# Attention overlapped with a narrow FFN1: where the additions, casts and loads of its inputs stand

## The chip, the cores and the metric

The kernel runs on one core of one Trainium2 chip. The metric is the device time of one launch in microseconds, lower is better. PE is TensorE, DVE VectorE, ACT ScalarE, POOL GpSimd; SP issues most transfers.

## The reference

```python
# attention: q, k, v are (4, 8, 576, 64); M_prev (4, 8, 64, 64); z_prev (4, 8, 64)
scores = where(causal, -1e9, q @ k.T / sqrt(64))
local = softmax(scores) @ v
q_p = elu(q) + 1
mem_out = (q_p @ M_prev) / (q_p . z_prev + 1e-06)
attn = g * mem_out + (1 - g) * local             # g = sigmoid(beta), one per head
x = attn, heads joined                           # (2304, 512)
x = elu(x @ w1_in) @ w1_out                      # w_in (512, 2048), w_out (2048, 512)
out = leaky(x @ w2_in, 0.01) @ w2_out
```

All is float32. In the FFN each float32 operand is kept as a rounded high part and a low rest, and a product takes three matmuls: high x high, high x low, low x high.

## The kernel before, in words

**Attention.** It goes batch by batch (0 to 3), and in a batch by pairs of heads. `attention_units` writes a list of small units with a cost each: products of scores, transposes of the weights, products with v, and the preparation of the next pair. Batch 0 leaves its result in one scratch array (`xm`). From batch 1 on a pair's result comes in two parts, and each goes through `xp` (DVE, line 529) and a store on SP (line 530) to `xq`; x is the sum of the two parts.

**The narrow part.** Seven of the sixteen blocks of 128 hidden columns of FFN1 run beside attention, for a batch whose attention is done. Its 576 tokens are cut into two halves of 288. A half is a row of units from `phase1_units`:

- `u_x`: from `xm` (batch 0, line 675) or `xq` (lines 681 and 682) SP loads x and y; for `xq` four additions of 128 x 288 on DVE (line 684); four casts to the high part xh on ACT (`split_x`, line 608, in the profile under its helper's line 239) and four subtractions to the low part xl on POOL (line 609); two stores of them.
- `u_h`, seven times, called H below: twelve matmuls (`h_mm`, line 616), then elu on ACT and DVE (lines 628 to 630) and the split of its result (lines 241 and 623).
- `u_o`, four times, called O: 21 matmuls (`o_mm`, line 644), a copy, and the store of ys (line 697).

**The order.** The loop at the end of the code below runs attention's units and counts their cost in `pos`. When a batch's attention is done, its narrow units are put into `fill`, to start at `pos + DELAY`, and from there on each attention unit earns credit with which narrow units are run. They run under `tc.high_priority(offset=FILL_OFF)`, which lets the scheduler pull their instructions some places ahead in the engines' lists. What is left of `fill` when attention ends goes to `side` and is merged with the loading of further weights. Then come the wide part of FFN1 (nine blocks) and FFN2, which the change leaves as they are.

An engine runs its list in order: an instruction that waits holds all those behind it.

Of the kernel before, what the change touches and what calls it, by code (L numbers as in the profile page):

```python
# [8 lines left out]
F32 = mybir.dt.float32  # L9
# [3 lines left out]
ALU = mybir.AluOpType  # L13
# [6 lines left out]
def _f(ap):  # L20
    return ap.bitcast(F32)
# [3 lines left out]
def kernel(  # L25
# [14 lines left out]
    nc = tc.nc  # L40
# [4 lines left out]
    NKC = DM // P  # L45
    NF = DFF // P
    NFA = 7
# [4 lines left out]
    V32 = 1  # L52
# [4 lines left out]
    E_GH, E_WH, E_VH, E_MS, E_V32, E_XH, E_RS, E_Y = "V", "A", "V", "P", "P", "A", "P", "A"  # L57
# [7 lines left out]
    RESERVE = 60000.0  # L65
    EARLY = 150
    DELAY = 13000.0
    NHP = H // 2
    PSUM = bass.MemoryType.PSUM

# [71 lines left out]
    def tile_tok(t):  # L142
        b, ca, cb = t
        r0 = CH[ca][0]
        r1 = CH[cb - 1][0] + CH[cb - 1][1]
        return b * S + r0, r1 - r0

    def halves(n):
        return [(0, n)] if n <= 320 else [(0, n // 2), (n // 2, n // 2)]


    parts = [(i, o, w, tile_tok(t)[0] + o) for i, t in enumerate(tiles1) for o, w in halves(tile_tok(t)[1])]
    xm_scr = [dram.tile([P, NKC, tile_tok(t)[1]], F32, name=f"xm{i}") for i, t in enumerate(tiles1)]
    xq_scr = [
        [dram.tile([P, NKC, tile_tok(t)[1]], F32, name=f"xq{i}_{j}") for j in range(2)] for i, t in enumerate(tiles1)
    ]
    xp_scr = [[dram.tile([P, NKC, p[2]], F32, name=f"x{n}{i}") for i, p in enumerate(parts)] for n in "hl"]
# [8 lines left out]
        out=mask[:, 448:576], in_=mask[:, 448:576], pattern=[[-1, 128]], compare_op=ALU.is_ge,  # L166
        fill=-1e30, base=0, channel_multiplier=1,
# [36 lines left out]
    def bank(tag):  # L204
        return psum.tile([P, 512], F32, tag=tag, bufs=BANKS[tag], name=tag)
# [31 lines left out]
    def copy(eng, dst, src):  # L237
        if eng == "A":
            nc.scalar.copy(dst, src)  # L239
        else:  # L240
            (nc.vector if eng == "V" else nc.gpsimd).tensor_copy(dst, src)  # L241
# [8 lines left out]
    class Pair:  # L250


        def __init__(self, ti, hp):
# [6 lines left out]
            self.full_v = ti < V32  # L260
            self.pad = pads[(ti * NHP + hp) % 2]

# [285 lines left out]
    def attention_units():  # L548

        pairs = [Pair(ti, hp) for ti in range(len(tiles1)) for hp in range(NHP)]  # L550
        keys = [(pr, j, g) for pr in pairs for j in range(2) for g in pr.groups]
# [45 lines left out]
    NW = 288  # L597

    def mtile(tag, bufs, dt=F32, shape=None):
        shape = shape or (NW,)  # L600
        pool = pools.get(("own", tag), pools["mlp"])
        return pool.tile([P] + list(shape), dt, tag=tag, bufs=bufs, name=tag)

    def split_x(xt, w, par):
        xh = mtile(f"xh{par}", 1, F32R, (NKC, NW))[:, :, 0:w]
        xl = mtile(f"xl{par}", 1, F32R, (NKC, NW))[:, :, 0:w]
        for c in range(NKC):
            copy(E_XH, xh[:, c], xt[:, c])
            nc.gpsimd.tensor_tensor(out=xl[:, c], in0=xt[:, c], in1=_f(xh[:, c]), op=ALU.subtract)
        return xh, xl  # L610

    def h_mm(ph, wi, xh, xl):
        n_mm = 0
        for kc in range(NKC):
            for wj, xx in ((0, xh), (1, xh), (0, xl)):
                nc.tensor.matmul(ph, wi[:, wj, kc, :], xx[:, kc, :], start=n_mm == 0, stop=n_mm == 11)  # L616
                n_mm += 1
# [8 lines left out]
    def elu(ph, w):  # L626
        e = mtile("e", EB)[:, 0:w]
        nc.scalar.activation(out=e, in_=ph, func=AF.Relu, scale=-1.0)
        nc.scalar.activation(out=e, in_=e, func=AF.Exp, scale=-1.0)
        nc.vector.scalar_tensor_tensor(out=e, in0=e, scalar=-1.0, in1=ph, op0=ALU.add, op1=ALU.max)  # L630
        return g_split(e, w)
# [7 lines left out]
    def o_mm(py, fs, key, ec, gs, first, last, opens=True, closes=True):  # L639
        for f in fs:  # L640
            wo = wo_tiles[key, f]
            gh, gl = gs[f]
            for n_mm, (wj, gg) in enumerate(((0, gh), (1, gh), (0, gl))):
                nc.tensor.matmul(  # L644
                    py, wo[:, wj, ec * P:(ec + 1) * P], gg,
                    start=opens and f == first and n_mm == 0, stop=closes and f == last and n_mm == 2,
                )
# [5 lines left out]
    def h_bank():  # L653
        nonlocal n_ph
        n_ph += 1
        return bank("tp" if tail and n_ph % 2 else "pm")

    def phase1_units(ti):

        units = []  # L660
        for pi, (pt, o, w, _) in enumerate(parts):
            if pt != ti:
                continue
            st = {}

            def u_x(pi=pi, o=o, w=w, st=st):
                def split():
                    st["x"] = split_x(xt, w, pi % 2)
                    for n in range(2):
                        nc.sync.dma_start(xp_scr[n][pi], _f(st["x"][n]))  # L670
                    st["g"] = {}

                xt = mtile("x", 1, F32, (NKC, NW))[:, :, 0:w]
                if ti < V32:
                    nc.sync.dma_start(xt, xm_scr[ti][:, :, o:o + w])
                    split()
                    return
                x2 = mtile("y", 1, F32, (NKC, NW))[:, :, 0:w]
                for j in range(2):
                    ps, pz = slice(64 * j, 64 * j + 64), slice(64 - 64 * j, 128 - 64 * j)  # L680
                    nc.sync.dma_start(xt[ps], xq_scr[ti][j][ps, :, o:o + w])
                    nc.sync.dma_start(x2[ps], xq_scr[ti][j][pz, :, o:o + w])
                for c in range(NKC):
                    nc.vector.tensor_tensor(out=xt[:, c], in0=xt[:, c], in1=x2[:, c], op=ALU.add)
                split()

            def u_h(f, w=w, st=st):
                ph = h_bank()[:, 0:w]
                h_mm(ph, wi_tiles[0, f], *st["x"])
                st["g"][f] = elu(ph, w)  # L690

            def u_o(ec, pi=pi, w=w, st=st):
                py = bank("sc" if tail else "pm")[:, 0:w]
                o_mm(py, range(NFA), 0, ec, st["g"], 0, NFA - 1)
                y = mtile("st", 2)[:, 0:w]
                copy(E_Y, y, py)
                nc.sync.dma_start(y_scr[pi][:, ec], y)

            units.append((0, u_x))
            for f in range(NFA):  # L700
                units.append((HC * 12 * w / 2.4, lambda f=f, u=u_h: u(f)))
            for ec in range(NKC):
                units.append((3 * NFA * w / 2.4, lambda ec=ec, u=u_o: u(ec)))
        return units

    def merge(a, bu):
        ta = sum(c for c, _ in a) + 1.0
# [14 lines left out]
    def close_decode():  # L722
        wst_a.__exit__(None, None, None)
        pools["decode_bank"] = None
        pools["outer"] = tc.tile_pool(name="mlpx", bufs=1, reuse_waits="tile", side="left")
        early = pools["outer"].__enter__()
        for tag in ("x", "y", "xh0", "xl0"):
            pools["own", tag] = early
        pools["own"] = tc.tile_pool(name="mlp", bufs=1, reuse_waits="tile", side="left")
        pools["mlp"] = pools["own"].__enter__()  # L730
# [17 lines left out]
    c_mlp = NFA * 24 * NT / 2.4  # L748
    rate = (c_mlp - RESERVE) / (c_att - DELAY)
    dec = [lambda f=f: load_w(0, wpa, w1i, w1o, f, f) for f in range(NFA)]  # L750
    fill = []
    credit = pos = 0.0
    for c, u, done in att:
        u()
        pos += c
        while dec and pos >= c0 * DSPAN * (NFA - len(dec)) / NFA:
            with tc.high_priority(offset=0):
                dec.pop(0)()
        if done == 0:
            close_decode()  # L760
        if done is not None:
            fill += [(pos + DELAY, c2, u2) for c2, u2 in phase1_units(done)]
        if fill and fill[0][0] <= pos:
            credit += c * rate
        while fill and fill[0][0] <= pos and fill[0][1] <= credit:
            _, c2, u2 = fill.pop(0)
            credit -= c2
            with tc.high_priority(offset=FILL_OFF):
                u2()
# [95 lines left out]
    for gi, (t0, w) in enumerate(wide):  # L865
        pos = {}
# [24 lines left out]
        for tb in range(w // P):  # L891
            r0 = t0 + tb * P
            for hf in range(2):
                cs = slice(hf * DM // 2, (hf + 1) * DM // 2)
                o = mtile("st", 2, F32, (DM // 2,))
# [32 lines left out]
```

## Time and profile before

| | |
|---|---|
| median of 3 runs | 1095.66 us (1095.63 to 1100.39) |
| profiled execution | 1098.26 us, span 1096.2 us, mean granted clock 0.995 |
| PE busy with matmuls | 1057.6 us (96%), 5904 matmuls |
| PE loading weights | 912.7 us (83%) |
| DVE / ACT / POOL busy | 600.3 us (55%) / 484.8 us (44%) / 530.6 us (48%) |

Attention fills the first 400 us or so, and the narrow part stands between its units from about 120 us on. The times of the trace below belong to the profiled execution, which took 2.6 us longer than the median.

### The profile page before, as it was taken

The numbers are of one execution on the slowest core, as the hardware profiler recorded it, in microseconds if no ns is written. First come the engines' busy times: TensorE is split into PE (matmuls) and PEld (weight loads), VectorE is DVE, ScalarE is ACT, GpSimd is POOL, SyncE is SP. The second block draws the span as 40 slices with busy tenths as digits, with TensorE's granted clock in tenths as the row PEclk, the third lists the DMA queues.
The fourth block names the chain that finished last, engine by engine and source line by source line (L and its number), as shares of the span: only waits on it lengthen the run. The fifth ranks groups of instructions, "written<-read, shape, count | busy, mean of one in ns | idle before, by whom it ended". The sixth has DMA issues, their size and how long they took to land.

```text
span 1096.2 us, 17406 instructions
## 1 busy us (share of the span) xinstructions
PE 1057.6 (96%) x5904; PEld 912.7 (83%) x5904; DVE 600.3 (55%) x1398; ACT 484.8 (44%) x1169; POOL 530.6 (48%) x674
## 2 busy tenths in 40 slices
PE   6998899989998999999999999999999999999997
PEld 3777789979998999978877889888888888888896
DVE  6889987778878857566574314664321222232232
ACT  5988877777877645444343223432211110111110
POOL 7675675667667626455453224755422322222221
PEclk9999999999999999999999999999999999999999
DMA  7753643564365139665653304331200100010010
GB/s 181 189 144 91 188 115 99 124 169 145 78 178 156 59 81 271 225 215 185 219 189 119 98 18 116 135 116 39 77 1 1 58 20 1 1 39 1 1 39 20
DMA packets 151576, 115.05 MB, mean 105 GB/s; under 512 B 81728, under 2 KB 144192, under 8 KB 151488
## 3 DMA queue, kind: packets, MB, share of 16 engines
q1 hardware_dynamic: 151488, 113.95, 35.5%
q8 instruction: 47, 0.77, 0.3%
q14 instruction: 41, 0.34, 0.1%
HBM read 78.52 MB, written 31.85 MB: 101 GB/s over the span
## 4 chain that ended last, share of the span: by engine, by line
PE 73%; DMA 8%; DVE 7%; POOL 3%; ACT 3%; SPq 3%; issue 3%; DVEq 0%; POOLq 0%; ACTq 0%
PE pm L616 17%; PE sc L876 14%; PE tp L616 13%; PE sc L644 8%; PE po L876 4%; PE pm L644 4%; PE po L522 3%; PE tp L455 3%; PE po L644 2%; DMA wraw<-in_moe_w_out_dram 2%; DMA x<-xq 2%; SPq L212 2%; PE sc L426 1%; PE sc L427 1%; PE pm L522 1%
## 5 line engine op out<-in xcount | busy, mean ns | idle before, releaser
L623 POOL TENSOR_TENSOR gl<-e,gh 128x512 fp32r<-128x512 f32 (+2 forms) x181 | 199.8, 1108 | 369.8 <-DVE gh L241 291.9
L616 PE MATMUL tp<-xw,w 128*128 128x512 f32 (+1 forms) x504 | 145.4, 371 | 0.9 <-DVE e L630 0.9
L616 PE MATMUL pm<-xw,w 128*128 128x512 f32 (+1 forms) x496 | 143.9, 371 | 0.0
L876 PE MATMUL sc<-w,gh 128*128 128x512 f32 x448 | 137.7, 393 | 0.0
L449 POOL TENSOR_SCALAR pt<-pt,rs,omg 128x128 f32<-128x128 f32 (+4 forms) x160 | 102.7, 651 | 28.0 <-DVE rs L444 25.7
L616 PEld LDWEIGHTS tp<-xw,w 128*128 128x128 f32 x504 | 91.3, 188 | 19.7 <-DVE e L630 1.7
L644 PE MATMUL sc<-gh,w 128*128 128x512 f32 (+2 forms) x438 | 106.0, 343 | 1.1 <-DVE st L857 0.7
L616 PEld LDWEIGHTS pm<-xw,w 128*128 128x128 f32 x496 | 90.5, 188 | 18.5
L434 ACT ACTIVATE pt<-pt,mx 128x128 f32<-128x128 f32 (+4 forms) x160 | 93.2, 585 | 22.7 <-DVE mx L429 22.1
L876 PEld LDWEIGHTS sc<-w,gh 128*128 128x128 f32 x448 | 83.1, 188 | 17.9
L616 PE MATMUL tp<-xv,w 128*128 128x512 f32 (+1 forms) x252 | 93.2, 370 | 0.0
L616 PE MATMUL pm<-xv,w 128*128 128x512 f32 (+1 forms) x248 | 92.0, 371 | 0.0
L616 PE MATMUL pm<-xh,w 128*128 128x288 f32 x368 | 80.2, 305 | 9.1 <-DVE e L630 5.7
L635 ACT ACTIVATE e<-pm 128x512 f32<-128x512 f32 (+1 forms) x40 | 22.2, 556 | 150.3 <-PE pm L616 149.1
L455 PE MATMUL tp<-ident,pt 128*128 128x128 f32 x480 | 80.1, 276 | 8.0 <-DVE al L248 3.1
L241 DVE CAST gh<-e 128x512 fp32r<-128x512 f32 (+2 forms) x146 | 77.9, 537 | 16.9 <-PE po L644 4.2
L137 POOL TENSOR_TENSOR w<-wm,w 128x512 fp32r<-128x512 f32 x50 | 66.1, 1344 | 43.4 <-ACT w L239 43.4
L876 PE MATMUL sc<-w,gl 128*128 128x512 f32 x224 | 85.4, 393 | 0.0
L644 PEld LDWEIGHTS sc<-gh,w 128*128 128x128 f32 x438 | 74.6, 188 | 12.2 <-issue 1.5
L636 DVE TENSOR_TENSOR e<-tp,e 128x512 f32<-128x512 f32 (+1 forms) x40 | 25.5, 637 | 107.2 <-ACT e L635 107.1
L636 DVE TENSOR_TENSOR e<-pm,e 128x512 f32<-128x512 f32 (+1 forms) x40 | 25.5, 637 | 105.8 <-ACT e L635 105.8
L429 DVE CUSTOM_DVE_ANT_0 pt<-sc,mask 128x128 f32<-128x128 f32 (+4 forms) x160 | 69.4, 446 | 8.6 <-PE sc L427 4.3
(155 smaller groups left out, 2407.9 us busy)
## 6 DMA issues: line engine op xcount, KB each, us to landing
wraw<-in_moe_w_in_dram SPq DMA_DIRECT2D x32, 512.0 KB, 4.1
wraw<-in_moe_w_out_dram SPq DMA_DIRECT2D x32, 512.0 KB, 5.3
xh<-xh SPq DMA_DIRECT2D x8, 576.0 KB, 3.3
xl<-xl SPq DMA_DIRECT2D x8, 576.0 KB, 3.9
ys<-st SPq DMA_DIRECT2D x32, 144.0 KB, 3.0
x1s<-st SPq DMA_DIRECT2D x36, 128.0 KB, 1.9
x<-x1s SPq DMA_DIRECT2D x9, 512.0 KB, 3.9
out_dram<-st SPq DMA_DIRECT2D x36, 128.0 KB, 1.7
```

The lines of the kernel that those rows point to most:

```text
L137: nc.gpsimd.tensor_tensor(out=w[:, 1, a], in0=t[:, a], in1=_f(w)[:, 0, a], op=ALU.subtract)
L241: (nc.vector if eng == "V" else nc.gpsimd).tensor_copy(dst, src)
L429: nc.vector.tensor_tensor_reduce(out=pt[0:m, k0:k0 + n], in0=sc[0:m, 0:n], in1=mk, op0=ALU.add, op1=ALU.min, scale=-0.125, scalar=mx[0:m, ...
L434: nc.scalar.activation(out=pt[0:m, 0:nk], in_=pt[0:m, 0:nk], func=AF.Exp, scale=-1.0, bias=mx[0:m, last:last + 1], accum_out=self.pd["ss"] ...
L449: nc.gpsimd.tensor_scalar(out=pt, in0=pt, scalar1=rs[0:m, i:i + 1], scalar2=omg[0:m, h:h + 1], op0=ALU.mult, op1=ALU.mult,)
L455: nc.tensor.transpose(dst, self.p[c][:, k0:k0 + kn], ident)
L522: nc.tensor.matmul(po[:, a:b], w, x, start=i == 0, stop=i == len(mms) - 1)
L616: nc.tensor.matmul(ph, wi[:, wj, kc, :], xx[:, kc, :], start=n_mm == 0, stop=n_mm == 11)
L623: nc.gpsimd.tensor_tensor(out=gl, in0=g, in1=_f(gh), op=ALU.subtract)
L636: nc.vector.tensor_tensor(out=t, in0=ph, in1=t, op=ALU.max)
L644: nc.tensor.matmul(py, wo[:, wj, ec * P:(ec + 1) * P], gg, start=opens and f == first and n_mm == 0, stop=closes and f == last and n_mm == 2,)
L876: nc.tensor.matmul(pos[tb], gg[:, tb * P:(tb + 1) * P], wo[:, wj, :], start=f == 0 and n_mm == 0, stop=f == NF - 1 and n_mm == 2,)
```

## The change

The loads of a half (`u_load`) are parted from its additions, casts and subtractions (`u_x`). The first half's loads are issued where the batch's attention ends, outside the raised priority. The second half's loads come after the second H unit of the first half, and its `u_x` after the sixth. The addition and the cast of c = 0 are held with `tc.keep_in_program_order` behind whatever was written before them for their engine; those of c = 1 to 3 stay free. From batch 1 on the narrow units start at `pos + LATE` with LATE = 20000, not at `pos + DELAY` with 13000; batch 0 keeps DELAY. The instructions and transfers stay the same in number and size.

```diff
--- before.py
+++ after.py
@@ -65,6 +65,7 @@
     RESERVE = 60000.0
     EARLY = 150
     DELAY = 13000.0
+    LATE = 20000.0
     NHP = H // 2
     PSUM = bass.MemoryType.PSUM
 
@@ -605,7 +606,9 @@
         xh = mtile(f"xh{par}", 1, F32R, (NKC, NW))[:, :, 0:w]
         xl = mtile(f"xl{par}", 1, F32R, (NKC, NW))[:, :, 0:w]
         for c in range(NKC):
-            copy(E_XH, xh[:, c], xt[:, c])
+            hi = nc.scalar.copy(xh[:, c], xt[:, c])
+            if c == 0:
+                tc.keep_in_program_order(hi)
             nc.gpsimd.tensor_tensor(out=xl[:, c], in0=xt[:, c], in1=_f(xh[:, c]), op=ALU.subtract)
         return xh, xl
 
@@ -657,32 +660,33 @@
 
     def phase1_units(ti):
 
-        units = []
-        for pi, (pt, o, w, _) in enumerate(parts):
-            if pt != ti:
-                continue
-            st = {}
-
-            def u_x(pi=pi, o=o, w=w, st=st):
-                def split():
-                    st["x"] = split_x(xt, w, pi % 2)
-                    for n in range(2):
-                        nc.sync.dma_start(xp_scr[n][pi], _f(st["x"][n]))
-                    st["g"] = {}
-
-                xt = mtile("x", 1, F32, (NKC, NW))[:, :, 0:w]
-                if ti < V32:
-                    nc.sync.dma_start(xt, xm_scr[ti][:, :, o:o + w])
-                    split()
-                    return
-                x2 = mtile("y", 1, F32, (NKC, NW))[:, :, 0:w]
-                for j in range(2):
-                    ps, pz = slice(64 * j, 64 * j + 64), slice(64 - 64 * j, 128 - 64 * j)
-                    nc.sync.dma_start(xt[ps], xq_scr[ti][j][ps, :, o:o + w])
-                    nc.sync.dma_start(x2[ps], xq_scr[ti][j][pz, :, o:o + w])
+        mine = [(pi, o, w, {}) for pi, (pt, o, w, _) in enumerate(parts) if pt == ti]
+
+        def u_load(pi, o, w, st):
+            xt = st["t"] = mtile("x", 1, F32, (NKC, NW))[:, :, 0:w]
+            if ti < V32:
+                nc.sync.dma_start(xt, xm_scr[ti][:, :, o:o + w])
+                return
+            x2 = st["t2"] = mtile("y", 1, F32, (NKC, NW))[:, :, 0:w]
+            for j in range(2):
+                ps, pz = slice(64 * j, 64 * j + 64), slice(64 - 64 * j, 128 - 64 * j)
+                nc.sync.dma_start(xt[ps], xq_scr[ti][j][ps, :, o:o + w])
+                nc.sync.dma_start(x2[ps], xq_scr[ti][j][pz, :, o:o + w])
+
+        def u_x(pi, o, w, st):
+            xt = st["t"]
+            if ti >= V32:
                 for c in range(NKC):
-                    nc.vector.tensor_tensor(out=xt[:, c], in0=xt[:, c], in1=x2[:, c], op=ALU.add)
-                split()
+                    add = nc.vector.tensor_tensor(out=xt[:, c], in0=xt[:, c], in1=st["t2"][:, c], op=ALU.add)
+                    if c == 0:
+                        tc.keep_in_program_order(add)
+            st["x"] = split_x(xt, w, pi % 2)
+            for n in range(2):
+                nc.sync.dma_start(xp_scr[n][pi], _f(st["x"][n]))
+            st["g"] = {}
+
+        units = [(0, lambda: u_x(*mine[0]))]
+        for k, (pi, o, w, st) in enumerate(mine):
 
             def u_h(f, w=w, st=st):
                 ph = h_bank()[:, 0:w]
@@ -696,12 +700,15 @@
                 copy(E_Y, y, py)
                 nc.sync.dma_start(y_scr[pi][:, ec], y)
 
-            units.append((0, u_x))
             for f in range(NFA):
                 units.append((HC * 12 * w / 2.4, lambda f=f, u=u_h: u(f)))
+                if k + 1 < len(mine) and f == 1:
+                    units.append((0, lambda k=k: u_load(*mine[k + 1])))
+                if k + 1 < len(mine) and f == NFA - 2:
+                    units.append((0, lambda k=k: u_x(*mine[k + 1])))
             for ec in range(NKC):
                 units.append((3 * NFA * w / 2.4, lambda ec=ec, u=u_o: u(ec)))
-        return units
+        return lambda: u_load(*mine[0]), units
 
     def merge(a, bu):
         ta = sum(c for c, _ in a) + 1.0
@@ -759,7 +766,10 @@
         if done == 0:
             close_decode()
         if done is not None:
-            fill += [(pos + DELAY, c2, u2) for c2, u2 in phase1_units(done)]
+            fetch, more = phase1_units(done)
+            fetch()
+            start = pos + (DELAY if done < V32 else LATE)
+            fill += [(start, c2, u2) for c2, u2 in more]
         if fill and fill[0][0] <= pos:
             credit += c * rate
         while fill and fill[0][0] <= pos and fill[0][1] <= credit:
```

What moves is read from the engines' lists; the lines of the changed kernel are one to four higher than those before (684 has become 680).

**DVE, first half of batch 1, before.** `sc` are scores, `pt` and `mx` the attention weights and their row maxima, `dl` and `al` low parts of transposed weights.

```order
L429 ISA mx 128x1
L429 ISA pt_3387,mx<-sc,mask,mx 128x288
L429 ISA mx 128x1
L684 TENSOR_TENSOR x<-x,y 128x288 x4
L529 COPY xp<-po 128x256
L444 RECIPROCAL rs<-rs 128x3
L429 ISA pt_3472,mx<-sc,mask 128x256
L429 ISA mx 128x1
```

**DVE, after,** where the three unpinned additions stand, and then where the pinned one does:

```order
L430 ISA pt_3202,mx<-sc,mask,mx 128x288
L430 ISA mx 128x1
L249 TENSOR_TENSOR dl_138<-tp,dh_136 128x384
L680 TENSOR_TENSOR x<-x,y 128x288 x3
L445 RECIPROCAL rs<-rs 128x3
L342 TENSOR_TENSOR qs_3228<-sc,qs_3228 64x256
L342 TENSOR_TENSOR qs_3228<-sc,qs_3228 64x320
L249 TENSOR_TENSOR ac<-tp,ac 64x320
```

```order
L430 ISA pt_3763,mx<-sc,mask 128x448
L430 ISA mx 128x1
L680 TENSOR_TENSOR x<-x,y 128x288
L390 TENSOR_REDUCE den<-ph_e 128x10
L430 ISA pt_3786,mx<-sc,mask 128x288
```

The four stood in a row. Now three stand some 30 rows further ahead among attention's instructions than the four did, and the first stands 77 rows behind them. The point of the last fence is, by its attention instructions, the one at which DVE was at 240.56 us in the trace before.

**SP, same place, before:**

```order
L530 DMA xq_1_87<-xp 128x320
L299 DMA kk_3154<-kk_3154 64x256
L299 DMA kk_3154<-kk_3154 64x320
L299 DMA kk_3155<-kk_3155 64x256
L299 DMA kk_3155<-kk_3155 64x320
L212 DMA kn<-in_k_dram 128x3x64
L212 DMA kn<-in_k_dram 128x2x64 x2
L212 DMA vn<-in_v_dram 128x2x64 x4
L217 DMA vn<-in_v_dram 64x2x64 x2
L230 DMA mr<-in_M_prev_dram 64x4x64 x2
L697 DMA ys_109<-st 128x288 x2
L530 DMA xq_0_88<-xp 128x256
L212 DMA qn<-in_q_dram 128x3x64 x2
L212 DMA qn<-in_q_dram 128x2x64 x2
L227 DMA zb<-in_z_prev_dram 128x256
L681 DMA x<-xq_1_87 64x4x288
L682 DMA y<-xq_1_87 64x4x288
```

**SP, after:**

```order
L531 DMA xq_1_87<-xp 128x256
L231 DMA mr<-in_M_prev_dram 64x4x64 x2
L701 DMA ys_109<-st 128x288
L300 DMA kk_3160<-kk_3160 64x256
L531 DMA xq_1_87<-xp 128x320
L300 DMA kk_3161<-kk_3161 64x256
L300 DMA kk_3160<-kk_3160 64x320
L673 DMA x<-xq_1_87 64x4x288
L674 DMA y<-xq_1_87 64x4x288
L300 DMA kk_3161<-kk_3161 64x320
L213 DMA kn<-in_k_dram 128x3x64 x2
L213 DMA kn<-in_k_dram 128x2x64 x2
L213 DMA vn<-in_v_dram 128x2x64 x4
L218 DMA vn<-in_v_dram 64x2x64 x2
```

The loads of x and y stood behind the loads of kn, vn and qn for the next pairs, and now stand ahead of those of kn and vn, close behind the last store of xq_1.

**PE, end of batch 0's narrow part, before.** `pm<-gh` are O, `pm<-xh` is H.

```order
L644 MATMUL pm<-gh,w_904 128x288 x2
L644 MATMUL pm<-gl,w_904 128x288
L644 MATMUL pm<-gh,w_1009 128x288 x2
L644 MATMUL pm<-gl,w_1009 128x288
L616 MATMUL pm<-xh_3624,w_200 128x288 x2
L522 MATMUL po<-qph,ms_164 128x320
L522 MATMUL po<-qpl,ms_164 128x320
L522 MATMUL po<-ah,vv 128x320 x2
```

**PE, after,** the end of O and then the first H:

```order
L427 MATMUL sc<-kk_3160,qs_3228 128x256
L428 MATMUL sc<-kl_1_175,qs_3228 128x256
L647 MATMUL pm<-gh,w_904 128x288
L647 MATMUL pm<-gl,w_904 128x288
L647 MATMUL pm<-gh,w_1009 128x288 x2
L647 MATMUL pm<-gl,w_1009 128x288
L456 MATMUL tp<-ident,pt_182 128x128
L523 MATMUL po<-qph,ms_164 128x256
L523 MATMUL po<-qpl,ms_164 128x256
L523 MATMUL po<-dh_152,vv 128x256 x2
```

```order
L456 MATMUL tp<-ident,pt_3584 128x128
L427 MATMUL sc<-kk_3564,qs_3636 128x256
L428 MATMUL sc<-kl_0_162,qs_3636 128x256
L427 MATMUL sc<-kk_3564,qs_3636 128x256
L428 MATMUL sc<-kl_0_162,qs_3636 128x256
L619 MATMUL pm<-xh_3774,w_200 128x288 x2
```

The first H followed the last O directly; between them now stand attention's matmuls alone.

## Rows read from the trace of the kernel before

**Rows 1.** The page, busy times and the chain that ended last.

```profile
PE 1057.6 (96%) x5904; PEld 912.7 (83%) x5904; DVE 600.3 (55%) x1398; ACT 484.8 (44%) x1169; POOL 530.6 (48%) x674
...
PE 73%; DMA 8%; DVE 7%; POOL 3%; ACT 3%; SPq 3%; issue 3%; DVEq 0%; POOLq 0%; ACTq 0%
```

**Rows 2.** Windows of 50 us: start:end, length, busy us (instructions) by engine, clock.

```profile
200.00:250.00 50.00, 44.58 (x324) 42.38 (x323) 38.66 (x116) 36.30 (x101) 31.20 (x49) 0.97 0.64 161
250.00:300.00 50.00, 50.00 (x390) 49.69 (x390) 40.92 (x130) 40.40 (x117) 33.02 (x56) 1.00 0.38 102
300.00:350.00 50.00, 46.05 (x345) 45.21 (x344) 40.05 (x115) 37.15 (x105) 35.30 (x54) 0.97 0.66 178
350.00:400.00 50.00, 48.93 (x376) 47.44 (x375) 37.26 (x110) 31.59 (x89) 24.96 (x40) 1.00 0.18 55
```

**Rows 3.** Waits of PE, whole span: waiter <- releaser: us in total, times, longest.

```profile
PE pm L616 <- DVE e L630: 5.7, 3, 2.8
...
PE pm L616 <- ACT xh L239: 3.4, 2, 1.8
```

**Rows 4.** Timeline of PE: start, length, engine, line, operation [idle before <- releaser].

```profile
121.37 0.81 PE L616 MATMUL pm<-xh,w 128*128 128x288 f32 x4 [1.85 <-ACT xh L239]
...
123.73 0.44 PE L337 MATMUL sc<-ident,qn 128*128 128x128 f32 x2 [0.40 <-DVE mx L429]
...
222.27 0.53 PE L616 MATMUL pm<-xh,w 128*128 128x288 f32 x2 [1.52 <-ACT xh L239]
...
244.50 0.53 PE L616 MATMUL pm<-xh,w 128*128 128x288 f32 x2 [2.59 <-DVE e L630]
...
323.68 0.52 PE L455 MATMUL tp<-ident,pt 128*128 128x128 f32 x3 [1.12 <-DVE al L248]
...
338.16 0.85 PE L616 MATMUL pm<-xh,w 128*128 128x288 f32 x2 [2.83 <-DVE e L630]
```

**Rows 5.** Timeline of SP, POOL and DVE around the first half of batch 1.

```profile
199.72 0.32 SPq L530 DMA_DIRECT2D xq<-xp  x1
200.14 2.50 SPq L299 DMA_DIRECT2D kk<-kk  x4
...
207.85 1.97 SPq L230 DMA_DIRECT2D mr<-in_M_prev_dram  x2
209.91 1.02 SPq L697 DMA_DIRECT2D ys<-st  x2
...
214.71 0.61 SPq L682 DMA_DIRECT2D y<-xq  x1
...
200.43 0.32 POOL L374 TENSOR_TENSOR ms<-mr,ms 64x64 fp32r<-64x64 f32 x1
...
205.89 0.56 DVE L248 TENSOR_TENSOR dl<-tp,dh 128x384 fp32r<-128x384 f32 x1
...
221.29 2.17 DVE L684 TENSOR_TENSOR x<-x,y 128x288 f32<-128x288 f32 x4 [4.79 <-issue]
```

**Rows 6.** Window 100 to 120 us, attention alone (columns as in rows 2).

```profile
100.00:120.00 20.00, 16.78 (x112) 13.71 (x110) 19.24 (x62) 15.03 (x44) 13.75 (x25) 1.00 0.50 126
```

**Rows 7.** Landing times of line 682 (y) and of line 530 (stores to xq).

```profile
DMA to landing us min/median/max: 4.0/4.6/9.6
...
DMA to landing us min/median/max: 1.7/2.0/6.3
```

**Rows 8.** Timeline of DVE: the additions of three other halves.

```profile
243.25 0.83 DVE L684 TENSOR_TENSOR x<-x,y 128x288 f32<-128x288 f32 x2 [2.07 <-DMA x<-xq]
...
320.03 0.83 DVE L684 TENSOR_TENSOR x<-x,y 128x288 f32<-128x288 f32 x2 [2.38 <-DMA y<-xq]
...
335.18 2.16 DVE L684 TENSOR_TENSOR x<-x,y 128x288 f32<-128x288 f32 x4 [2.87 <-DMA y<-xq]
```

**Rows 9.** Two windows of 5 us behind the idle time at 244.50.

```profile
245.00:250.00 5.00, 5.00 (x30) 4.87 (x29) 5.00 (x16) 3.71 (x10) 5.00 (x8) 0.66 0.40 152
250.00:255.00 5.00, 5.00 (x39) 4.93 (x39) 3.73 (x15) 4.38 (x15) 3.65 (x7) 1.00 0.44 159
```

## The prediction, made before the changed kernel ran

> **What bounds the kernel now.** Page, busy shares: PE is busy for 96% of the span, and the chain that ended last lies 73% on it and 7% on DVE [rows 1]. A gain must come from places where PE could have issued and did not, so I read next the busy time by stretches of 50 us. One stretch is saturated: 390 matmuls from 250 to 300 us, which is 7.8 in a us. The two beside it hold 324 and 345, and the last of attention 376 [rows 2]. The waits of PE name the narrow part as the largest causes: the first product of an H unit waits 5.7 us for DVE's elu and 3.4 us for ACT's cast xh [rows 3]. The timeline of PE shows where: 1.85 us at 121.37 (batch 0), 1.52 at 222.27 and 2.59 at 244.50 (batch 1), 1.12 and 2.83 at 323.68 and 338.16 (batch 2) [rows 4].
>
> The reason is on DVE and SP. Four additions stand in a row in DVE's list. In batch 1 DVE reaches them after 216.5 and sits idle 4.79 us until 221.29, since SP issued the load of y only at 214.71 [rows 5]. Everything behind them in DVE's list, attention's row maxima and the elu included, stands still, and PE runs dry. In the other halves DVE idles 2.07, 2.38 and 2.87 us before them [rows 8].
>
> **The change, part by part.** No instruction is added or removed; 24 additions, 32 casts and all transfers stay. Only places move.
>
> *Loads earlier.* In SP's list the last x and y of batch 1's first half now stand two kk copies behind the last store of xq_1, ahead of the loads of kn and vn, not behind them. In the trace's time: POOL is done with the old ms at 200.75, which frees mr; the two mr take 1.97 us, a ys 0.51, a kk copy 0.62; the last xq store is issued near 203.9 and lands 2.0 later, two more kk copies beside it; x goes at 205.9, y at 206.5, against 214.12 and 214.71 [rows 5, 7]. Landing takes 4.6 us (median; 4.0 to 9.6) [rows 7]: 211.1. The kn and vn loads that stand behind move back by some 4 us; the transposes of kn come at 224.84, so I cost this at nothing. If that slack were gone, PE would wait for kn by up to those 4 us.
>
> *Three of four additions early, the pinned one late.* Only c = 0 is pinned; the other three are still pulled ahead, to behind the dl that DVE starts at 205.89 [rows 5]. DVE comes there at about 206.4, the data at 211.1: a wait of 4.7 us. Behind it stand rs, qs and ac of attention. PE has some 30 O matmuls left there, 30 x 0.128 = 3.8 us (50 us over 390 [rows 2]), so 0.9 us shows. Batch 2 has the same pattern and a wait of 2.38 before [rows 8]; under O matmuls it costs 0.1. Second halves: their loads go out after H unit 1 and the additions after H unit 5. Four H units are 48 matmuls, 6.2 us, and a landing takes 4.6: nothing. **Waits: 1.0 us**, bounds 0 and the four waits of before, 4.79 + 2.07 + 2.38 + 2.87 = 12.1.
>
> *The gain.* The pinned addition stands late, behind attention's instructions that before stood behind the four, and the casts follow it. What PE lost there by count of matmuls against 390: batch 1 has 66 fewer, 66 / 7.8 = 8.5 us; batch 2 has 45 fewer, 5.8; the last 50 us of attention, into which the later O units now fall, 14 fewer, 1.8 [rows 2]. In batch 0 the idle of 1.85 and the 0.40 at 123.73 are covered by 26 attention matmuls moved ahead of the first H product: 2.25 [rows 4]. Sum **18.35 us**. The low bound goes by idle time alone: 5.42 + 3.95 + 1.07 + 2.25 = 12.7 [rows 2, 4]. I take the count, because it holds the half-speed clock too: after the 2.59 us idle at 244.50 the granted clock averages 0.66 over 5 us (part at 1.2 GHz, the rest at 2.4), with 30 matmuls where the next 5 us hold 39 [rows 9]: 1.2 us that no idle row shows.
>
> The Trainium skill, Perfetto Trace Analysis, § Identifying the Most-Contended Engine, says that matmul busy time is a poor measure of nearness to the limit, and weight-load busy time a good one. By it batch 1 lost 49.69 - 42.38 = 7.3 us, batch 2 4.5 and the last stretch 2.25; the sum would be 16.3, and the forecast 2 us nearer to before. The trace sides with the count or the loads over busy PE: 42.38 of weight loads stand beside 44.58 of PE in one stretch, 49.69 beside 50.00 in the full one [rows 2].
>
> *The price of LATE.* Between the last O of batch 0 and the first H of batch 1 nothing of the narrow part stood before; now 148 attention matmuls stand there alone (counted in PE's order), in batch 2 71, and in batch 0 the 26 above. Attention alone is in the trace at 100 to 120 us: 112 matmuls in 20 us, 5.6 in a us, with DVE busy for 19.24 of 20 [rows 6]. DVE is the bound there, and PE's free 3.2 us are lost since the narrow products come later, in time that PE alone fills. At 5.6 and not 7.8 in a us: 148 take 26.4 for 19.0, 7.4 lost; 71 lose 3.6; 26 lose 1.3. **12.3 us**. The low bound goes by the idle share, 3.22 of 20: 0.161 x (26.4 + 12.7 + 4.6) = 7.0. I take the count again, the measure in which the gain was read. Three O units more come after attention; their matmuls only change place. The kn, vn, mr and store issues on SP keep their number, and POOL's subtractions follow the casts as before.
>
> **Sum.** -18.35 + 12.3 + 1.0 = -5.05 us. The profiled execution took 1098.26 (span 1096.2), 2.6 above the median of 1095.66; it would become 1093.2, and against the median the forecast is **1090.6 us**. A measurement of this kernel can tell about 0.5% from no change: below 1090.2 is faster, above 1101.1 slower. The forecast lies at the edge of what can be told.
>
> **Rivals.** (a) *The gaps go and DVE has slack.* DVE was busy for only 38.66 of 50 us in batch 1 [rows 2], so the alone stretch may run better than at 100 us, where it also carried batch 1's preparation. Then it costs the low bound, 7.0, and the waits nothing: -18.35 + 7.0 = -11.35, 1084.3. Against it: 19.24 of 20 [rows 6].
>
> (b) *It doesn't do what it says.* The pin holds one addition of four; three go ahead and DVE stands at them as it stood at four. The idle of PE goes by its low bound, 12.7, and the alone stretches take 12.3 of it: 1095.66 - 12.7 + 12.3 + 1.0 = 1096.3, no change. For it: the order shows the three ahead in every half of batches 1 and 2.
>
> (c) *Slower: DVE's new wait falls where DVE is the bound.* The early three stand some 10 us earlier in DVE's list than the four did, their loads issue 8.2 us earlier, and the stretch behind has no narrow product to cover for DVE. If y lands after its longest, 9.6 us [rows 7], DVE waits 9.7 us in batch 1, 5.9 beyond the O matmuls; batch 2 and the second halves keep their 2.38, 2.07 and 2.87 [rows 8], bare; and two idles of that length lower the clock as the one at 244.50 did, 1.2 each [rows 9]. Sum 5.9 + 7.3 + 2.4 = 15.6 in place of 1.0: -18.35 + 12.3 + 15.6 = +9.6, 1105.2. It decides once the uncovered waits pass 6 us. Against it: the median landing; the cover in batch 2.
>
> The Trainium skill, Perfetto Trace Analysis, § Optimization Strategy, says that stretches with different limiting engines may gain from being interleaved. LATE does the reverse, a DVE-bound stretch apart from PE-bound products, so by that rule (c) has the better of it; the trace agrees that the limits differ, 19.24 of 20 us on DVE at 100 and 50.00 of 50 on PE at 250 [rows 6, 2].
>
> **How the numbers follow.** Forecast 0.48 (its spread 1086 to 1094: 0.26 beyond the bound, 0.22 within), (a) 0.15, (b) 0.18, (c) 0.19. Faster 0.26 + 0.15 = 0.41; same 0.22 + 0.18 = 0.40; slower 0.19. The range reaches from just under (a), 1083, to 1103, which leaves out most of (c) beyond its middle and little at the low end.
>
> **What would show it.** Right: in the profile after, PE's waits for the cast xh and the elu e fall from 9.1 us to under 2; the stretch 200 to 250 holds some 350 matmuls, fewer per us in 205 to 230 and full after; DVE waits some 4.7 us once at the early additions of batch 1, with PE busy on O beside it. (b): PE's idle stays within 2 us of before in sum. (c): PE idles over 2.5 us near 210 and the clock drops behind it. The forecast is wrong if the alone stretch shows PE at over 7 matmuls in a us (faster than forecast), or if the second halves still show waits for y.

## The result, and the profile after

| | before | changed |
|---|---|---|
| median of 6 runs | 1096.62 us (1095.46 to 1100.39) | 1106.11 us (1103.27 to 1109.16) |
| ratio, 95% interval | | 1.0073 [1.0053, 1.0093] |
| profiled execution | 1098.26 us, span 1096.2 | 1103.41 us, span 1101.5 |

The changed kernel is slower by 0.7%, some 8 us. The forecast was 1090.6, faster by 0.5%, and its range ended at 1103. The profiled execution of the changed kernel is one of its faster ones; its span shows 5.3 us of the loss.

The page of the changed kernel, busy times and the chain, against [rows 1]:

```profile
PE 1063.4 (97%) x5904; PEld 915.5 (83%) x5904; DVE 591.8 (54%) x1398; ACT 484.8 (44%) x1169; POOL 528.5 (48%) x674
...
PE 78%; DVE 7%; DMA 5%; ACT 3%; issue 3%; POOL 3%; SPq 1%; DVEq 0%; ACTq 0%; POOLq 0%
```

PE is busier in time with the same 5904 matmuls, so the sum of busy time doesn't tell where it went. The windows do (columns as in [rows 2]):

```profile
200.00:250.00 50.00, 45.24 (x321) 41.14 (x319) 43.62 (x130) 35.21 (x100) 32.15 (x53) 0.97 0.61 159
250.00:300.00 50.00, 49.14 (x375) 47.91 (x375) 42.73 (x131) 42.22 (x122) 34.04 (x54) 1.00 0.45 124
300.00:350.00 50.00, 45.55 (x341) 43.03 (x340) 42.42 (x126) 36.82 (x106) 32.31 (x51) 1.00 0.42 102
350.00:400.00 50.00, 49.19 (x376) 48.27 (x375) 30.41 (x89) 31.09 (x86) 25.93 (x39) 1.00 0.39 124
400.00:450.00 50.00, 45.58 (x322) 44.31 (x321) 28.17 (x46) 24.28 (x48) 25.85 (x26) 0.97 0.73 228
```

From 200 to 400 us little moved: 324, 390, 345 and 376 matmuls have become 321, 375, 341 and 376 [rows 2], 22 fewer in all, or 2.8 us at 7.8 in a us; beside batch 0, from 100 to 150, there are 9 more, 306 for 297. The larger loss shows from 400 to 450, after attention, where the kernel before had 361:

```profile
400.00:450.00 50.00, 48.50 (x361) 47.80 (x360) 30.22 (x50) 24.54 (x53) 27.37 (x30) 1.00 0.87 266
```

39 matmuls at 7.8 in a us are 5.0 us. The waits of PE between 200 and 460 us in the changed kernel (waiter <- releaser: total, times, longest):

```profile
PE sc L427 <- DVE qs L342: 3.3, 2, 2.5
PE sc L427 <- DVE mx L430: 3.3, 3, 1.6
PE tp L619 <- ACT xh L609: 2.6, 1, 2.6
PE po L523 <- DVE xp L530: 2.4, 5, 0.7
...
PE pm L619 <- POOL xl L612: 0.8, 1, 0.8
...
PE pm L619 <- DVE e L633: 0.2, 1, 0.2
```

The waits of [rows 3], 9.1 us for the elu and the cast, are gone from `pm`, over the whole span too: 0.2 for e, 0.8 for xl. That part of the forecast came true. In their place stand attention's own waits for DVE (qs, mx, xp: 9.0 us; in the same stretch of the kernel before only xp, 1.3), and one of 2.6 us for xh at `tp`, the bank that H uses only after attention. ACT at that place:

```profile
409.91 1.17 ACT L609 CAST xh<-x 128x288 fp32r<-128x288 f32 x3 [4.02 <-DVE x L680]
411.72 1.14 ACT L127 ACTIVATE wm<-wraw 128x1024 f32<-128x1024 f32 x1 [0.64 <-DMA wraw<-in_moe_w_out_dram]
412.77 0.68 ACT L240 COPY st<-sc 128x288 f32<-128x288 f32 x2
416.14 1.04 ACT L240 CAST w<-wm 128x1024 fp32r<-128x1024 f32 x1 [2.69 <-DVE wm L132]
417.60 0.83 ACT L240 COPY st<-sc 128x288 f32<-128x288 f32 x2 [0.42 <-DMA ys<-st]
418.33 0.43 ACT L609 CAST xh<-x 128x288 fp32r<-128x288 f32 x1
```

This is the first half of batch 3. Three casts run at 409.91, as soon as the additions are done. The held one, c = 0, stands behind what was written before it for ACT: the weight preparation, which waits 2.69 us for DVE, and the copies of the last O units. It runs 8 us after the others, and the first matmul of H is the one that reads it. In the kernel before all four stood ahead of the weight preparation:

```profile
412.59 1.17 ACT L239 CAST xh<-x 128x288 fp32r<-128x288 f32 x3 [3.14 <-DVE x L684]
414.31 0.43 ACT L239 CAST xh<-x 128x288 fp32r<-128x288 f32 x1 [0.55 <-DVE x L684]
416.83 1.14 ACT L126 ACTIVATE wm<-wraw 128x1024 f32<-128x1024 f32 x1 [2.09 <-DMA wraw<-in_moe_w_in_dram]
```

In the changed kernel PE starves, and its clock falls:

```profile
418.82 0.82 PE L619 MATMUL tp<-xh,w 128*128 128x288 f32 x2 [2.56 <-ACT xh L609]
```

```profile
415.00:420.00 5.00, 2.44 (x15) 2.21 (x14) 1.11 (x1) 2.39 (x5) 2.74 (x3) 0.89 0.90 244
420.00:425.00 5.00, 5.00 (x32) 5.00 (x32) 3.51 (x4) 2.40 (x5) 0.52 (x1) 0.77 1.02 398
425.00:430.00 5.00, 5.00 (x39) 5.00 (x39) 2.09 (x5) 2.57 (x6) 3.87 (x4) 1.00 1.04 289
```

The clock averages 0.77 in the 5 us behind, between 1.2 and 2.4 GHz, and 7 matmuls fewer are issued than in the next 5.

So the first theory, T: the hold costs after attention, where nothing of attention stands beside it. Its rivals: L, all the loss is LATE's stretch of attention alone; P, the three additions that run ahead hold DVE. A second question is why nothing was gained up to 400 us.

### The profile page after: what moved, and what is told of

Read it like the earlier page. It is cut to its first block, busy times and chain, and to the rows that moved or that the text cites. A ratio compares the mean times of both kernels' runs of the same rounds, so it can differ in the third digit from the quotient of the medians.

```text
span 1101.5 us, 17413 instructions
## 1 busy us (share of the span) xinstructions
PE 1063.4 (97%) x5904; PEld 915.5 (83%) x5904; DVE 591.8 (54%) x1398; ACT 484.8 (44%) x1169; POOL 528.5 (48%) x674
## 4 chain that ended last, share of the span: by engine, by line
PE 78%; DVE 7%; DMA 5%; ACT 3%; issue 3%; POOL 3%; SPq 1%; DVEq 0%; ACTq 0%; POOLq 0%
PE pm L619 18%; PE tp L619 15%; PE sc L886 14%; PE sc L647 9%; PE po L886 4%; PE pm L647 4%; PE po L523 4%; PE tp L456 3%; PE po L647 2%; DMA x<-xq 2%; PE sc L427 1%; PE sc L428 1%; DVE pt L430 1%; PE pm L523 1%; SPq L213 1%
## 5 line engine op out<-in xcount | busy, mean ns | idle before, releaser
L647 PE MATMUL sc<-gh,w 128*128 128x512 f32 (+2 forms) x466 | 112.4, 340 | 0.7 <-DVE gh L242 0.6
L435 ACT ACTIVATE pt<-pt,mx 128x576 f32<-128x576 f32 (+4 forms) x160 | 93.2, 585 | 27.9 <-DVE mx L430 26.1
L647 PEld LDWEIGHTS sc<-gh,w 128*128 128x128 f32 x466 | 78.9, 188 | 11.5 <-DVE gh L242 0.8
L242 DVE CAST gh<-e 128x512 fp32r<-128x512 f32 (+2 forms) x146 | 72.2, 497 | 22.0 <-PE po L647 7.0
L638 ACT ACTIVATE e<-tp 128x512 f32<-128x512 f32 (+1 forms) x40 | 22.1, 553 | 117.7 <-PE tp L619 117.5
```

The source lines that it names most:

```text
L435: nc.scalar.activation(out=pt[0:m, 0:nk], in_=pt[0:m, 0:nk], func=AF.Exp, scale=-1.0, bias=mx[0:m, last:last + 1], accum_out=self.pd["ss"] ...
L638: nc.scalar.mul(t, ph, 0.01)
L647: nc.tensor.matmul(py, wo[:, wj, ec * P:(ec + 1) * P], gg, start=opens and f == first and n_mm == 0, stop=closes and f == last and n_mm == 2,)
```

## Experiments

Ratios are to the kernel before, with their 95% intervals. In the diffs the base is the changed kernel unless said otherwise.

**Holds only while attention runs.**

```diff
-            if c == 0:
+            if c == 0 and attending:
                 tc.keep_in_program_order(hi)
...
-                    if c == 0:
+                    if c == 0 and attending:
                         tc.keep_in_program_order(add)
```

> The changed kernel with the addition and the cast of c = 0 held in place only while attention is running, so that batch 3's two halves, which come after attention, are free again. Theory T (the held cast of batch 3 stands on ACT behind the stores' copies and the weight casts, and PE starves): the 2.6 us wait of PE for xh near 418 and the smaller gaps to 443 go; about 3 to 5 us less than the changed kernel, ratio to the kernel before about 1.003 to 1.004. Theory L (all of the loss is the stretch of attention alone that LATE makes): as the changed kernel, about 1.007.

Measured: 1.0007 [0.9989, 1.0024], span 1094.8. T holds, and the hold after attention costs more than the 3 to 5 us expected: 1.0073 less 1.0007 is 0.66%, some 7 us. ACT and the window:

```profile
408.88 1.17 ACT L609 CAST xh<-x 128x288 fp32r<-128x288 f32 x3 [3.65 <-DVE x L680]
410.61 0.43 ACT L609 CAST xh<-x 128x288 fp32r<-128x288 f32 x1 [0.55 <-DVE x L680]
411.59 1.15 ACT L127 ACTIVATE wm<-wraw 128x1024 f32<-128x1024 f32 x1 [0.55 <-DMA wraw<-in_moe_w_out_dram]
```

```profile
400.00:450.00 50.00, 48.61 (x364) 48.15 (x363) 32.93 (x50) 25.80 (x54) 28.55 (x29) 1.00 0.81 258
```

All four casts stand ahead of the weight work, and the window holds 364 matmuls, not 322. L as the whole explanation falls.

**LATE back at 13000, holds everywhere.** Diff: `LATE = 20000.0` becomes `13000.0`.

> The changed kernel with LATE = 13000, so that the narrow units of batch 1 on start where they did before. Theory L: the stretch of attention alone goes, the time falls by 7 us or more, to 1.000 or under it. Theory T: the halves of batch 3 lose as much as in the changed kernel, some 3 to 5 us, so the ratio stays at 1.003 or more. Theory P (the three additions that float ahead and hold DVE): no change, 1.007.

Measured: 1.0047 [1.0034, 1.0060]. The hold after attention keeps its price here too: PE waits 1.9 us for xh, and the window from 400 to 450 holds 318 matmuls. Against the changed kernel LATE is worth 0.3% (the two intervals overlap), not the whole.

```profile
400.00:450.00 50.00, 45.08 (x318) 43.67 (x317) 25.48 (x42) 22.98 (x47) 25.41 (x27) 0.97 0.77 240
```

**No holds at all,** early loads and LATE as in the change. Diff: both `if c == 0:` with their line left out.

> The changed kernel without both holds (early loads and LATE = 20000 stay). Theory T: the loss at batch 3 goes, 3 to 5 us; but all four additions float ahead together, so nothing of DVE's early wait is saved: ratio 1.003. Theory L: as the changed kernel, 1.007. If the hold of c = 0 is what removed PE's waits for the narrow inputs in attention, then waits for xh and e come back by up to 9 us: 1.010 or more.

Measured: 1.0059 [1.0043, 1.0076]. T's 1.003 and the 1.010 were missed; L's 1.007 lies in the interval, but the first run had ruled L out as the whole. What is won after attention is lost in it: PE waits 4.7 us for attention's qpl, where the first run has 0.7. Beside the first run the only difference is the hold during attention, and it is worth 0.5%; its addition and its cast were not tried apart there. So the hold is right in one place and wrong in the other.

**LATE alone, on the kernel before.**

```diff
+    LATE = 20000.0
...
-            fill += [(pos + DELAY, c2, u2) for c2, u2 in phase1_units(done)]
+            start = pos + (DELAY if done < V32 else LATE)
+            fill += [(start, c2, u2) for c2, u2 in phase1_units(done)]
```

> The kernel before with LATE = 20000 alone: loads, additions and casts stay in one unit, nothing is held. Theory L: this alone is slower, by the stretch of attention alone, 7 to 12 us less whatever it still covers of the waits: 1.004 to 1.010. Theory T: LATE alone costs little, within 2 us, 1.000 to 1.002, since the loss sits in the held cast of batch 3.

Measured: 0.9990 [0.9973, 1.0008], no change. On the kernel before the later start costs nothing in sum; it is not a fixed price, then. But PE's waits for the cast and the elu fell with it, from 9.1 us [rows 3] to 3.3, with no hold and no early load:

```profile
PE pm L617 <- ACT xh L240: 2.4, 2, 1.4
...
PE pm L617 <- DVE e L631: 0.9, 2, 0.5
```

So the nothing may be a price and a gain that cancel, and the fall of these waits is no gain in time by itself. The profiled execution, span 1097.2, holds a stall of another kind beside batch 0's narrow part, where LATE does not apply: PE waits 4.94 us at 127.28 for one DVE cast that took 6.35 us (last section). Whether the timed runs had it too is not known, so LATE alone may be worth a little more than the ratio says.

**LATE = 13000 and holds only while attention runs** (the first two edits together).

> The changed kernel with LATE = 13000 and the holds only while attention runs. If LATE's stretch of attention alone costs what it gained in covered waits (theory L, in its smaller form), this is faster than the same kernel with 20000 (1.0007) by 3 to 5 us and than the kernel before: 0.996 to 0.998. If the stretch costs nothing of its own, it stays at 1.000 or above.

Measured: 0.9970 [0.9949, 0.9990]. As expected: faster than before, and 0.4% below the same kernel with 20000, though the two intervals touch.

**All four additions and casts held while attention runs, LATE = 20000.**

```diff
-            if c == 0:
+            if attending:
                 tc.keep_in_program_order(hi)
...
-                    if c == 0:
+                    if attending:
                         tc.keep_in_program_order(add)
```

> LATE = 20000, and while attention runs all four additions and casts are held, not c = 0 alone; free after attention. If the three that float ahead hold DVE and so PE (2.5 to 3.3 us idle at 307, 0.9 at 214 in the trace), this is faster than with c = 0 alone (1.0007) by 3 to 4 us: 0.997. If their wait is hidden, or if the first products now wait for four late casts, 1.000 to 1.002.

Measured: 1.0022 [1.0005, 1.0040]. The 0.997 was missed; the value lies at the edge of the other branch, and that is the end of P as the cause of the loss. The additions of attention now wait for nothing, but with LATE = 20000 that brings no time: the first H of batch 1 comes at 238.73, after a stretch of attention alone.

**The same with LATE = 13000.**

> As the run with all four held, but LATE = 13000. If both costs are real and add, the fastest of all, 0.993 to 0.995. If all four held at the earlier place wait bare for their loads, as in the kernel before, 1.000.

Measured: 0.9962 [0.9944, 0.9979], the lowest of the ratios, span 1092.3, and a little less gain than the 0.993 to 0.995 expected. Its interval overlaps with that of c = 0 alone held (0.9970), so that three more holds bring time is not shown. Against the run before it LATE is worth 0.6%, with intervals well apart. Between 200 and 400 us no idle time of DVE stands before any of its 16 additions, and batch 1's window is fuller than in any of the runs above:

```profile
226.90 1.56 DVE L680 TENSOR_TENSOR x<-x,y 128x288 f32<-128x288 f32 x4
```

```profile
200.00:250.00 50.00, 47.54 (x354) 46.17 (x353) 40.86 (x127) 37.51 (x109) 32.90 (x52) 0.97 0.58 149
```

354 matmuls against 324 before, 3.8 us at 7.8 in a us: this is the gain that the forecast looked for, at the place it looked.

**Only the cast free after attention;** the addition of c = 0 stays held there.

```diff
-            if c == 0:
+            if c == 0 and attending:
                 tc.keep_in_program_order(hi)
```

> The changed kernel with only the cast of c = 0 set free after attention; the addition of c = 0 stays held there too. If the loss after attention is the cast's place on ACT, nearly all of it goes: 1.001 to 1.002. If the held addition on DVE is part of it (it stands behind the weight preparation on DVE in batch 3's second half), half of it stays: 1.003 to 1.005.

Measured: 1.0016 [1.0001, 1.0031]. Of the 0.0066 between the changed kernel and holds in attention only, 0.0057 goes with the cast alone; the rest is within the intervals. Nearly all of the loss after attention is the place on ACT of the held casts, one in each half of batch 3.

**Early loads without holds:** LATE = 13000, and the second half's `u_x` stays after the sixth H unit, as in the change.

> Early loads alone: the changed kernel without holds and with LATE = 13000. If the holds are what makes the early loads pay while attention runs, this is slower than with them (0.997), at 1.000 to 1.004, with DVE idle before the additions as in the run without holds. If the loads' place alone does it, 0.997.

Measured: 1.0043 [1.0026, 1.0059]. Without the holds the early loads, and the earlier place of the second half's additions and casts that came with them, make the kernel slower; the two were not tried apart. DVE and PE in batch 1, first half:

```profile
214.89 2.17 DVE L678 TENSOR_TENSOR x<-x,y 128x288 f32<-128x288 f32 x4 [1.82 <-issue]
216.98 0.48 DVE L249 TENSOR_TENSOR qpl<-po,qph 128x320 fp32r<-128x320 f32 x1
```

```profile
217.51 0.39 PE L523 MATMUL po<-qph,ms 128*128 128x256 f32 x1 [3.81 <-DVE qpl L249]
```

The four additions, free to move, stand ahead of attention's qpl. DVE waits 1.82 us and spends 2.17 on them (the row names no load, but y was issued at 210.04, and these loads land in 3.8 to 4.8 us); PE waits 3.81 us for the qpl behind. Here it is an attention product that stands still, not a narrow one.

**All four held, LATE = 8000.**

> All four held while attention runs, LATE = 8000. If attention alone costs by its length, another 2 to 3 us go against LATE = 13000 (0.9962): 0.993 to 0.995. If the additions then come to DVE before their loads have landed, DVE waits bare again and the gain is given back: 0.997 or above.

Measured: 0.9981 [0.9962, 1.0000]. No better than 13000, as far as the intervals tell; the window from 200 to 250 holds the same 354 matmuls. The additions come no earlier than with 13000, at 227.86 us against 226.90, and no idle time of DVE stands before them, so the bare wait that was expected of the other branch is not what stopped the gain. Shorter than 13000 brings nothing more.

Put side by side (early loads, with the second half's `u_x` after the sixth H, in all but the last row):

| held in attention | held after it | LATE | ratio |
|---|---|---|---|
| c = 0 | c = 0 (the change) | 20000 | 1.0073 |
| c = 0 | c = 0 | 13000 | 1.0047 |
| c = 0 | addition only | 20000 | 1.0016 |
| c = 0 | none | 20000 | 1.0007 |
| c = 0 | none | 13000 | 0.9970 |
| none | none | 20000 | 1.0059 |
| none | none | 13000 | 1.0043 |
| all four | none | 20000 | 1.0022 |
| all four | none | 13000 | 0.9962 |
| all four | none | 8000 | 0.9981 |
| none, loads not early | none | 20000 | 0.9990 |

## Why the prediction was wrong

**The step that failed first: the hold was priced in batches 1 and 2 only.** The text followed the held addition and the casts behind attention's instructions and said that "the casts follow it" at no cost. The change holds c = 0 in batch 3 as well. There ACT's list holds weight preparation and stores, whose own waits the cast inherits. Of the stretch after attention the text says only that three more O units come there and "their matmuls only change place". The term was not in the sum; it measured 0.66% (1.0073 against 1.0007), some 7 us, and 0.77% with LATE = 13000 (1.0047 against 0.9970). The profiled execution shows 5.0 us of it, the window from 400 to 450. Rows of ACT's list for the first half of batch 3, with the cast of c = 0 behind copies that wait for O, could have shown it beforehand.

**The gain of 18.35 us was mis-sized.** It took every matmul that was missing against a full window for one lost to the narrow waits. Those waits did go, 9.1 us to 1.0 on `pm`. But the window of batch 1 holds 321 matmuls where some 350 were forecast, and in the run with LATE alone the same waits fell by 5.8 us with no gain in time. (The 1.12 us at 323.68 that the text lists among the narrow waits is a wait of attention's transpose for al [rows 4].) DVE's idle 4.79 us had not been the only limit: the early additions hold attention instead. Batch 2 shows it. DVE and PE of the changed kernel:

```profile
308.89 1.20 DVE L680 TENSOR_TENSOR x<-x,y 128x288 f32<-128x288 f32 x3 [1.78 <-DMA vn<-in_v_dram]
310.12 0.49 DVE L342 TENSOR_TENSOR qs<-sc,qs 64x320 fp32r<-64x320 f32 x1
```

```profile
310.67 0.47 PE L427 MATMUL sc<-kk,qs 128*128 128x448 f32 x1 [2.53 <-DVE qs L342]
...
311.18 0.50 PE L619 MATMUL pm<-xh,w 128*128 128x288 f32 x2
```

Three early additions, a wait of 1.78 us and 1.20 of work, stand ahead of qs, and PE waits 2.53 us for it. The forecast had 0.1 here, "under O matmuls". That cover failed in a way the rows show: the scores product stands ahead of the narrow matmuls in PE's list, and what stands behind a waiting instruction covers nothing. In batch 1 the cover held: SP issued y at 204.26, DVE waited 1.79 us until 208.94, not the 4.7 forecast, and PE lost next to nothing before 214 us. A second half waits too, where the forecast had nothing, in batch 2; PE then idles 0.80 us for the qs behind:

```profile
359.40 1.20 DVE L680 TENSOR_TENSOR x<-x,y 128x288 f32<-128x288 f32 x3 [1.92 <-DMA x<-xq]
```

With holds in attention only and LATE = 13000, early loads and holds together gained 0.3%, some 3 us, where the forecast had 17 before the price of LATE. With all four held it is 0.4%. Why the rest of the 18.35 us did not come is not shown; what is shown is that the end of those waits does not bring it.

**The price of LATE had the right rate and was no fixed sum.** Attention alone between the last O of batch 0 and the first H of batch 1:

```profile
210.00:239.60 29.60, 25.49 (x167) 21.77 (x167) 27.74 (x85) 22.91 (x65) 19.69 (x33) 0.94 0.45 116
```

167 matmuls in 29.6 us are 5.6 in a us, as forecast from [rows 6], with DVE busy for 27.74 of 29.6. But of the 12.3 us 11.0 are for batches 1 and 2, to which LATE applies, and that was two to three times too high: LATE costs 0.4%, some 4 us, with c = 0 held in attention, 0.6% with all four, about 0.2% without holds (intervals overlap), and nothing measurable on the kernel before. So gain and price were not two things to add. A likely reason is that both counted the same matmuls, which PE did not issue while DVE was the limit; that is argued, not shown.

Together, by the ratios: the hold after attention cost some 7 us that the sum left out, the gain fell some 13 us short (3 for 16, which is the 17 less 1.3 for batch 0's stretch), and LATE took some 7 us less (4 for 11). Their sum is the 13 us between the forecast and the result. Without the hold after attention the time would have been that of the kernel before (1.0007), inside the range, but only since the other two errors partly cancel.

**The rivals.** (c) came nearest in time, 1105.2 for 1106.1, by luck, and was wrong in its mechanism: it put the loss on waits of DVE at the early additions in batches 1 and 2 and PE idle near 210. DVE's waits there were short, 1.79, 1.78 and 1.92. (b) was right that three additions ahead of the held one keep part of the stall: holding all four took it away, though no gain in time from that is clear of the intervals.

The Trainium skill, Perfetto Trace Analysis, § Optimization Strategy, was cited with (c): interleaving stretches with different limits may help. The runs agree where all four are held, 0.9962 with the earlier start and 1.0022 with the later one; on the kernel before the later start changed nothing (0.9990).

## What to carry to other kernels

An instruction held in its place inherits the waits of everything written before it on that engine. Price a hold at each place where the code with it runs, the last batch above all, where another stage's work fills the list. And deficits that two views show in one stretch, idle behind a wait and a slow engine, can be the same microseconds: add them only if different windows hold them.

## What the runs showed that was not expected

**A DVE cast of 6.35 us beside a busy POOL.** In the run with LATE alone, DVE's cast of v, 128 x 320, stood for 6.35 us beside batch 0's narrow part; the 22 casts of this kind between 100 and 400 us have a median of 0.35. (The longest of the 22 takes 1.53 in the kernel before and 2.38 in the changed one.) DVE, then POOL:

```profile
120.50 6.35 DVE L242 CAST vv<-vn 128x320 fp32r<-128x320 f32 x1
```

```profile
119.51 2.31 POOL L450 TENSOR_SCALAR pt<-pt,rs,omg 64x320 f32<-64x320 f32 x3 [0.50 <-DVE rs L445]
121.80 0.79 POOL L610 TENSOR_TENSOR xl<-x,xh 128x288 fp32r<-128x288 f32 x1
122.58 0.98 POOL L450 TENSOR_SCALAR pt<-pt,rs,omg 128x128 f32<-128x128 f32 x2
123.54 2.28 POOL L610 TENSOR_TENSOR xl<-x,xh 128x288 fp32r<-128x288 f32 x3
125.79 0.85 POOL L366 TENSOR_TENSOR vv<-vn,vv 128x320 fp32r<-128x320 f32 x1
126.93 0.86 POOL L366 TENSOR_TENSOR vv<-vn,vv 128x320 fp32r<-128x320 f32 x1 [0.30 <-DVE vv L242]
```

POOL works without a break from 119.51 to 126.64, and the cast ends at 126.85, after it (times on POOL are rough). PE waited 4.94 us for a row maximum queued behind the cast. That POOL held the cast is inferred from these rows; no run tried it. The Trainium skill, GPSIMD Engine Reference, § 8 Key points, says that POOL shares its SBUF interfaces with DVE, and that they contend when the DVE instruction runs in a two-port mode or reads two inputs from SBUF. This cast reads one input, and no row shows its mode, so the rows fit the page only if it ran in such a mode. If POOL is the cause, the order of its list, which none of the views above looked at, can add some 5 us.

**Early loads.** Without holds the earlier loads, with the second half's earlier `u_x`, made the kernel slower by 0.4% (1.0043; y of batch 1 was issued at 210.04, not 214.71): the additions then stand ahead of attention's qpl, and PE idles 3.81 us at one place.

**Two late casts.** Two casts of 0.43 us each, one in each half of batch 3, cost some 6 us in the end (1.0073 against 1.0016): 2.56 us idle behind the first, a clock of 0.77 for the 5 us after it, and further gaps in batch 3 up to 445 us, where the windows still hold 34, 32 and 33 matmuls each 5 us:

```profile
430.00:435.00 5.00, 4.48 (x34) 4.25 (x33) 4.96 (x8) 3.38 (x8) 4.66 (x6) 1.00 0.03 12
435.00:440.00 5.00, 4.42 (x32) 4.03 (x31) 4.79 (x9) 2.94 (x6) 3.19 (x3) 1.00 0.18 53
440.00:445.00 5.00, 4.24 (x33) 4.00 (x32) 1.38 (x3) 1.13 (x1) 4.13 (x5) 1.00 0.89 340
```

Which part of these later gaps is the second half's held cast, at 439.42 on ACT, and which is the shift of the weight work, was not tried apart.
